# Loading a layer's last keys ahead of its last three values, with the last unit's turned probabilities in the place of the final piece of w_down

## The chip, the cores and the metric

The kernel runs on one core of one Trainium2 chip. TensorE (PE) multiplies, VectorE (DVE) transposes and reduces, ScalarE (ACT) takes exponentials, GpSimd (POOL) makes small tiles, and SyncE (SP) issues every DMA; the DMA engines bring data from HBM to SBUF. The metric is the device time of one execution in microseconds, as the median of several.

## The reference

Two layers, each a decode step of grouped-query attention and a SwiGLU feed-forward block, are applied to `x` of shape (4, 1, 512). Both layers use the same caches and weights:

```
x = x + attention(layernorm(x), k_cache, v_cache, wq, wo)
x = x + swiglu(layernorm(x), w_gate, w_up, w_down)
x = x + attention(layernorm(x), k_cache, v_cache, wq, wo)
x = x + swiglu(layernorm(x), w_gate, w_up, w_down)
```

There are 4 sequences, 32 query heads and 8 key/value heads of width 128, and 8192 cached positions. `attention` is `softmax(q k^T / sqrt(128)) v` followed by `wo`; `swiglu` is `(silu(x w_gate) * (x w_up)) w_down` with 1792 hidden columns. All inputs are bf16. The keys and the values hold 67 MB each, so that the two layers read some 270 MB, against which all weights are small.

## The kernel before, in words

**Units.** A layer has 16 units (`NP`); one unit is a pair of key/value heads of one sequence. Its keys are 4 MB (128 partitions by 16384 columns) and its values as many. Layer 0 takes the units in the order 0 to 15, layer 1 in the order 15, 14, 0, 1, ..., 13 (`order`, line 294), since the keys of unit 15 and the values of 14 and 15 stay in SBUF from one layer to the next (`keep`, line 392). K and V with a number are the keys and values of the unit at that place of its layer.

**Slots.** SBUF has four slots of 4 MB (`kv`, `NSLOT`). Keys, values and, at the end of a layer, the weights of the feed-forward block (`W`) take them in turn. A slot has eight parts. `cmds` (lines 300 to 332) is the list of all loads with their slots. `pump` (line 363) issues them from SP strictly in that order: a load whose slot is not free holds back all that follow. A slot becomes free part by part, as the products that read it are done (`finished`, `freed`). At the end of a layer the order of loads is K14, V13, K15, V14, the two halves of V15, W. In layer 0 W takes the slot of V13, and in layer 1 also the slot of V13. At the beginning of layer 1 the loads go in quarters and halves, so that they can start before a whole slot is free.

**Work on a unit's keys** (`keys`, line 495). DVE transposes each of the eight parts in place (`turn`, line 422). PE then multiplies each part with the placed queries, four products a part (`scores`, line 442), into one of two PSUM banks (`SBK`). When all eight are done come the steps of the softmax: the maximum over positions (`max_p`, line 448), its turn to one row and the reduction to eight heads (`max_t`, lines 452 and 455), the broadcast, bias and exponential (`exps`, lines 462 to 469, into the tile `pb`), the sum and its reciprocal (`total`, lines 478 and 480, into `rl`), and the transposes of the probabilities (`turn_p`, line 475, from `pb` to the tile `pT`).

**Work on a unit's values** (`values`, line 518). Four parts of eight products each (line 530) read `pT` and write one PSUM bank (`OBK`); two parts use up one half of the slot. Then DVE gathers the four quarters of that bank into `acc`, which lies in `pb` (`gather`, lines 546 and 549), PE combines the partitions (line 553), and DVE scales with `rl` (line 555). After the fourth unit of a group of heads, `out_proj` (line 570) multiplies with `wo` and adds to `x`.

**Order of the work.** The program order of all engines is made when the kernel is built. `blocks` holds the products of keys and values, each with a nominal duration, and `drain` (line 487) emits them with a lag behind the transposes. `line` holds the small steps, each with a gap that has to pass in blocks before it is emitted (`advance`). The exponential and what follows wait in `behind` until the values of the unit before are done (line 539), since `pT` and `pb` have one buffer each; `flush` (line 412) emits what is left of a unit's steps before its values. Line 699 sets the order K0, K1, V0, K2, V1, ..., K15, V14, V15. After it come `center`, `deviation` and `ffn`: the gate and up products (line 647), the activation, the down products in three pieces (line 666). The parts of W's slot become free after the gate products, the up products and the down products, and the keys of layer 1 go there.

`_Sync` (line 21) makes the semaphore waits: each operation names what it reads and writes, and waits for the last writers and readers of these names.

Of the kernel before, what the change touches and what calls it, by code (L numbers as in the profile page):

```python
# [103 lines left out]
def bass_interleave_layers__gqa_block_cached__swiglu_ffn__decode_kernel(  # L104
# [40 lines left out]
    with ExitStack() as es:  # L145
# [13 lines left out]
        W_SLOT = (0, 2)  # L159
# [22 lines left out]

        def room(s, a, b):
            return [f"s{s}.{q}" for q in range(a // BW, (b - 1) // BW + 1)]
# [115 lines left out]
        cmds = []  # L300
        us = order[0]
        seq = [K(0, us[0])]
        for i in range(1, NP):
            seq += [K(0, us[i]), V(0, us[i - 1])]
        seq.append(V(0, us[-1]))
        for i, it in enumerate(seq):
            cmds.append((it, i % NSLOT, 0, NB))
        where = {it: s for it, s, _, _ in cmds}
        last = cmds.pop()
        cmds += [(last[0], last[1], 0, NB // 2), (last[0], last[1], NB // 2, NB)]  # L310
        assert where[V(0, NP - 2)] == 2 and where[K(0, NP - 1)] == 1 and where[V(0, NP - 1)] == 3
# [7 lines left out]
        rest = []  # L319
        for i in range(3, NP):  # L320
            rest += [K(1, us[i]), V(1, us[i - 1])]
        rest.append(V(1, us[-1]))
        ring = (0, 3, 1, 2)
        for i, it in enumerate(rest):
            s = ring[i % NSLOT]
            if i in (0, 2):
                cmds += [(it, s, q, q + 2) for q in range(0, NB, 2)]
            elif i == 1 or i == len(rest) - 1:
                cmds += [(it, s, q, q + NB // 2) for q in range(0, NB, NB // 2)]
            else:  # L330
                cmds.append((it, s, 0, NB))
        cmds += [(("W", 1), W_SLOT[1], 0, NB)]

# [4 lines left out]
        def load_weight(name, i=0, s=0):  # L338
# [7 lines left out]
            else:  # L346
                w0 = kvf[:, s * SL:(s + 1) * SL]
                T.dma("sp", w0[:, 0:KT * F].rearrange("p (k f) -> p k f", k=KT),
# [9 lines left out]
                for j, (a, b) in enumerate(WD):  # L358
# [134 lines left out]
        behind = []  # L493

        def keys(L, u, alone, lag):
            def block(q):
# [21 lines left out]
        def values(L, u):  # L518
            gp, b = pair_gb(u)

            def part(i):
                if i == 0:
                    flush(u)
# [225 lines left out]
```

## Time and profile before

| what | value |
| --- | --- |
| median of 3 runs | 660.75 us (660.32 to 662.91) |
| the profiled execution | 663.07 us |
| its span on the core | 661.3 us |
| mean granted TensorE clock | 0.817 |
| PE, DVE, ACT, POOL busy | 65%, 64%, 6%, 2% of the span |
| DMA | 274.44 MB, mean 415 GB/s |
| the main DMA queue's packets | 97.9% of 16 engines' span |
| chain that ended last | DMA 56%, PE 19%, DVE 18%, issue 4% |

The chain that ended last is followed back from the last instruction: at each step it goes to what released that instruction. Its DMA part is the keys (`kvf<-in_A_k_cache_dram`). Times inside the profile count from the start of the span. A row of the timeline gives start, length, engine, line, operation, tiles and count, and in brackets the idle time of the engine before it and what ended it. A row of the windows gives the stretch, its length, the busy time (and count) of PE, PEld, DVE, ACT and POOL, the granted TensorE clock, the DMA share and GB/s.

### The profile page before, as it was taken

Reading aid. Unit: us, or ns where it says so; the run is one execution under the profiler, and the core shown is the slowest. Engines: PE = TensorE matmul, PEld = TensorE weight load, DVE = VectorE, ACT = ScalarE, POOL = GpSimd, SP = SyncE. Lnnn points to the kernel's source line nnn. Section 1 sums busy time; section 2 is a strip of 40 time slices with the busy share of each in tenths; the row PEclk is TensorE's granted clock in tenths of the full one; section 3 lists DMA queues with packets and bytes.
Section 4 is the critical chain, followed back from the end, with each engine's and each line's share of the span. In section 5 each row is a group of like instructions: output and inputs, shape, how many; then the busy total and the mean of one; then the engine's idle time right before and its main releaser. Section 6 shows DMA issues by size and latency. Waiting matters only on the chain.

```text
span 661.3 us, 7677 instructions
## 1 busy us (share of the span) xinstructions
PE 429.4 (65%) x3192; PEld 185.0 (28%) x3192; DVE 420.3 (64%) x701; ACT 38.6 (6%) x107; POOL 10.7 (2%) x43
## 2 busy tenths in 40 slices
PE   2575467465777655577657888677666568765576
PEld 2222123122223222233225342222322123222135
DVE  1675457566677666577644948867756667765673
ACT  1000000000000000000000000000000000000010
POOL 0000000000000000000000000000000000000000
PEclk9995797689887778987675969997767898777886
DMA  9999999999999999999998999999999999999994
GB/s 379 419 428 403 433 429 414 423 436 431 429 431 428 437 428 431 431 429 432 420 406 331 347 426 437 429 435 428 431 430 431 434 427 432 431 431 429 430 411 153
DMA packets 19522, 274.44 MB, mean 415 GB/s; under 512 B 1560, under 2 KB 5920, under 8 KB 9504
## 3 DMA queue, kind: packets, MB, share of 16 engines
q1 hardware_dynamic: 19488, 273.95, 97.9%
q8 instruction: 25, 0.41, 0.3%
q14 instruction: 9, 0.07, 0.0%
HBM read 273.94 MB, written 0.00 MB: 414 GB/s over the span
## 4 chain that ended last, share of the span: by engine, by line
DMA 56%; PE 19%; DVE 18%; issue 4%; another core or an unknown queue 1%; ACT 1%; SPq 0%; POOL 0%; ACTq 0%; DVEq 0%; POOLq 0%
DMA kvf<-in_A_k_cache_dram 56%; PE ps L442 12%; DVE kvf L422 11%; PE ps L530 2%; DVE pT L475 2%; DVE pb L549 2%; PE ps L570 1%; PE ps L647 1%; ACT pb L467 1%; PE ps L462 1%; PE ps L608 1%; PE ps L553 0%; DVE pb L546 0%; PE ps L666 0%
## 5 line engine op out<-in xcount | busy, mean ns | idle before, releaser
L442 PE MATMUL ps<-kvf,zq 128*128 128x512 bf16 x1024 | 306.3, 444 | 183.6 <-DVE kvf L422 179.8
L422 DVE STREAM_TRANSPOSE kvf<-kvf 128x1024 f32<-128x1024 f32 x248 | 293.1, 1216 | 157.0 <-DMA kvf<-in_A_k_cache_dram 156.9
L442 PEld LDWEIGHTS ps<-kvf,zq 128*128 128x128 bf16 x1024 | 97.4, 109 | 336.4 <-DVE kvf L422 231.4
L530 PE MATMUL ps<-kvf,pT 128*32 128x512 bf16 x1024 | 70.5, 399 | 12.3 <-DVE pT L475 12.3
L467 ACT ACTIVATE pb<-ps,tiny 128x512 bf16<-128x512 f32 x32 | 22.0, 687 | 577.2 <-DVE tiny L465 454.5
L475 DVE STREAM_TRANSPOSE pT<-pb 64x512 bf16<-64x512 bf16 x64 | 43.7, 682 | 1.1
L530 PEld LDWEIGHTS ps<-kvf,pT 128*32 128x32 bf16 x1024 | 23.8, 98 | 45.8 <-issue 28.7
L549 DVE SCALAR_TENSOR_TENSOR pb<-ps,tiny,pb 128x128 f32<-128x128 f32 x96 | 33.7, 351 | 3.4
L448 DVE TENSOR_REDUCE tiny<-ps 128x1 f32<-128x512 f32 x32 | 22.0, 689 | 4.7 <-PE ps L442 3.5
L553 PEld LDWEIGHTS ps<-sel,pb 128*128 128x128 f32 x64 | 17.8, 287 | 19.8 <-DVE pb L549 10.6
L455 DVE TENSOR_REDUCE m<-ps 1x8 f32<-1x128 f32 x32 | 8.8, 276 | 19.8 <-PE ps L452 19.8
L433 POOL TENSOR_TENSOR zq<-scr,tiny 128x64 bf16<-128x64 bf16 x32 | 9.6, 299 | 605.2 <-PE ps L442 523.8
L553 PE MATMUL ps<-sel,pb 128*128 128x8 f32 x64 | 12.9, 274 | 7.1 <-DVE pb L549 7.1
L546 DVE TENSOR_SCALAR pb<-ps,tiny 128x128 f32<-128x128 f32 x32 | 10.1, 315 | 9.6 <-PE ps L530 9.6
L478 PE MATMUL ps<-rsm,tiny 128*128 128x8 f32 x64 | 11.6, 254 | 6.0 <-ACT rsm L469 5.8
L478 PEld LDWEIGHTS ps<-rsm,tiny 128*128 128x128 f32 x64 | 10.6, 194 | 17.3 <-ACT rsm L469 16.0
L462 PEld LDWEIGHTS ps<-m,tiny 1*128 1x128 f32 x64 | 10.2, 198 | 17.1 <-issue 15.9
L462 PE MATMUL ps<-m,tiny 1*128 1x8 f32 x64 | 13.1, 274 | 0.2 <-DVE m L455 0.2
L608 PE MATMUL ps<-xn,wq_sb 128*128 128x4 bf16 x256 | 7.9, 166 | 4.8 <-DMA wq_sb<-in_A_wq_dram 4.7
L452 PE MATMUL ps<-identf,tiny 128*1 128x128 f32 x32 | 8.8, 273 | 1.9 <-DVE tiny L448 1.9
L469 ACT ACTIVATE rsm<-head,tiny 128x8 f32<-128x8 f32 x32 | 9.6, 301 | 1.0
L480 DVE RECIPROCAL rl<-ps 128x8 f32<-128x8 f32 x32 | 5.5, 172 | 6.2 <-PE ps L478 6.2
(61 smaller groups left out, 94.3 us busy)
## 6 DMA issues: line engine op xcount, KB each, us to landing
kvf<-in_A_k_cache_dram SPq DMA_DIRECT2D x27, 4096.0 KB, 26.9
kvf<-in_A_v_cache_dram SPq DMA_DIRECT2D x27, 4096.0 KB, 34.0
kvf<-in_A_v_cache_dram SPq DMA_DIRECT2D x6, 2048.0 KB, 26.3
kvf<-in_A_k_cache_dram SPq DMA_DIRECT2D x12, 1024.0 KB, 9.2
wq_sb<-in_A_wq_dram SPq DMA_DIRECT2D x4, 1024.0 KB, 7.9
wo_sb<-in_A_wo_dram SPq DMA_DIRECT2D x4, 1024.0 KB, 28.3
kvf<-in_B_w_gate_dram SPq DMA_DIRECT2D x2, 1792.0 KB, 29.0
kvf<-in_B_w_down_dram SPq DMA_DIRECT2D x4, 768.0 KB, 19.6
```

What stands on the lines that cost most here:

```text
L422: T.op("dve", lambda e: e.transpose(w, w), reads=[f"s{s}.{q}"], writes=[f"s{s}.{q}"])
L442: T.op("pe", lambda e: e.matmul(bank(bk)[:, 0:SW], lhsT=zq[:, z0:z0 + P], rhs=w[:, :, c // 2, :, c % 2], start=(q == 0 and c == 0), stop=( ...
L448: T.op("dve", lambda e: e.tensor_reduce(mx[:], bank(bk)[:, 0:SW], AX.X, ALU.max), reads=[f"pb{bk}"], writes=["mx"])
L462: T.op("pe", lambda e: e.matmul(bank(STEP)[:, 0:H2], lhsT=onesf[0:1, :].to_broadcast([1, P]), rhs=m8[:], start=True, stop=True), reads=["m ...
L467: T.op("act", lambda e: e.activation(pb[:], bank(bk)[:, 0:SW], ACTF.Exp, bias=nm, accum_out=rs), reads=[f"pb{bk}", "nm"], writes=PB + ["rs"])
L475: T.op("dve", lambda e: e.transpose(dst, pb[hp]), reads=["pb"], writes=["pT"])
L478: T.op("pe", lambda e: e.matmul(bank(TOT)[:, 0:H2], lhsT=ones, rhs=rsm[:], start=True, stop=True), reads=["rsm", "onesf"], writes=[f"pb{TO ...
L530: T.op("pe", lambda e: e.matmul(bank(OBK)[j * QB:(j + 1) * QB, :], lhsT=pT[:, t, h, :], rhs=v[:, :, t, :], start=first, stop=stop), reads= ...
L546: T.op("dve", lambda e: e.tensor_scalar(acc, o(0), own[:, 0:1], None, op0=ALU.mult), reads=[f"pb{OBK}", "own"], writes=PB)
L549: T.op("dve", lambda e: e.scalar_tensor_tensor(acc, o(q), own[:, q:q + 1], acc, op0=ALU.mult, op1=ALU.add), reads=[f"pb{OBK}", "own", "pb" ...
L553: T.op("pe", lambda e: e.matmul(bank(CMB)[:, 0:H2], lhsT=acc, rhs=sel[:], start=True, stop=True), reads=["pb", "sel"], writes=[f"pb{CMB}"])
L608: T.op("pe", lambda e: e.matmul(bank(LNB)[:, h * B:(h + 1) * B], lhsT=wq_sb[:, kt, h * Dh:(h + 1) * Dh], rhs=xn[:, kt * B:(kt + 1) * B], s ...
```

## The change

The last keys of a layer, K15, are loaded and multiplied ahead of V13, V14 and V15; before, V13 came ahead of K15 and V14 behind it. The list of loads ends in K14, K15, V13, V14, the halves of V15, W in both layers, and the work in K14, K15, V13, V14, V15 (`todo`). So K15 takes the slot that V13 had, and V13 that of K15; W has the slot of V13 in layer 0 (`W_SLOT` is 1) and of K15 in layer 1 (2). The slots of the loads at the start of layer 1 are renumbered to go with it.

The softmax steps of units 14 and 15 from `exps` on now both stand behind the values of unit 13. Two units' probabilities are then alive at once. Those of unit 15 get a second place: the last 1024 columns of W's slot (`late_pT`), which the last piece of w_down fills at the end of the layer. POOL clears that place, when what lay there is done with, and the last piece of w_down becomes a load of its own (`W+`), which waits for the values of unit 15 and stands on SP ahead of layer 1's first keys. The row of maxima `m8` and the reciprocals `rl` become two each.

```diff
-        W_SLOT = (0, 2)
+        W_SLOT = (1, 2)
...
+        pT_w = TB * NH * QB
+        def late_pT(s):
+            return kvf[:, (s + 1) * SL - pT_w:(s + 1) * SL]
...
-        m8 = sb("m8", [1, H2], FP32)
+        m8 = sb("m8", [1, 2, H2], FP32)
-        rl = sb("rl", [P, H2], FP32)
+        rl = sb("rl", [P, 2, H2], FP32)
...
+        def loads(L, first):
+            us = order[L]
+            seq = []
+            for i in range(first, NP - 1):
+                seq += [K(L, us[i]), V(L, us[i - 1])]
+            seq.insert(len(seq) - 1, K(L, us[NP - 1]))
+            return seq[:-2] + [seq[-2], seq[-1], V(L, us[NP - 2]), V(L, us[NP - 1])]
...
-        cmds += [(("W", 0), W_SLOT[0], 0, NB)]
+        cmds += [(("W", 0), W_SLOT[0], 0, NB), (("W+", 0), W_SLOT[0], NB, NB + 1)]
         us = order[1]
-        cmds += [(K(1, us[1]), 0, 0, 3), (K(1, us[1]), 0, 3, 4), (K(1, us[1]), 0, 4, NB)]
-        cmds += [(K(1, us[2]), 1, q, q + 2) for q in range(0, NB, 2)]
...
-        ring = (0, 3, 1, 2)
...
-        cmds += [(("W", 1), W_SLOT[1], 0, NB)]
+        s = W_SLOT[0]
+        cmds += [(K(1, us[1]), s, 0, 3), (K(1, us[1]), s, 3, 4), (K(1, us[1]), s, 4, NB)]
+        cmds += quarters(K(1, us[2]), 0)
+        seq = loads(1, 3)
+        cmds += placed(seq, (1, 3, 0, 2), {0: quarters, 1: half, 2: quarters, len(seq) - 1: half})
+        cmds += [(("W", 1), W_SLOT[1], 0, NB), (("W+", 1), W_SLOT[1], NB, NB + 1)]
...
+                if name == "W+":
+                    load_wd(w0, len(WD) - 1, ["late"])
+                    return
+                T._wait("pool", T._need((), [f"s{s}.{NB - 1}"]))
+                T.op("pool", lambda e: e.memset(late_pT(s).bitcast(FP32), 0.0), writes=["late"])
                 T.dma("sp", w0[:, 0:KT * F].rearrange("p (k f) -> p k f", k=KT),
...
-                for j, (a, b) in enumerate(WD):
-                    T.dma("sp", w0[:, O_WD + a * D:O_WD + b * D].rearrange("p (m x) -> p m x", x=2 * D),
-                          B_w_down[a * P:b * P, :].rearrange("(m p e) n -> p m (e n)", p=P, e=2), sem_w["wd"][j],
-                          writes=[f"wd{j}"])
+                for j in range(len(WD) - 1):
+                    load_wd(w0, j)
...
+        def pT_of(L, u):
+            if u == order[L][-1]:
+                return late_pT(W_SLOT[L]).rearrange("p (t n x) -> p t n x", n=NH, x=QB), "late"
+            return pT[:], "pT"
...
-                    behind.extend([step(0.9, exps), step(1.0, total), step(0.3, turn_p)])
-                    if alone:
-                        line.extend(behind)
-                        behind.clear()
+                    (line if before is None else behind.setdefault(before, [])).extend(
+                        [step(0.9, exps), step(1.0, total), step(0.3, lambda u: turn_p(L, u))])
...
                 if i == 0:
-                    flush(u)
+                    flush(order[L][-1] if u == order[L][-2] else u)
...
                 if i == 3:
+                    if p_name == "late":
+                        freed(W_SLOT[L], NB, NB + 1)
                     done.add((L, u))
                     line[0:0] = rest_
-                    line.extend(behind)
-                    behind.clear()
+                    line.extend(behind.pop(u, []))
...
-            for i, u in enumerate(us):
+            todo = [("K", 0)]
+            for i in range(1, NP - 1):
+                todo += [("K", i), ("V", i - 1)]
+            todo[-1:] = [("K", NP - 1)] + [("V", i) for i in range(NP - 3, NP)]
+            for kind, i in todo:
+                if kind == "V":
+                    values(L, us[i])
+                    continue
...
-                keys(L, u, i == 0, AHEAD if L and i in (1, 2) else LAG)
-                if i:
-                    values(L, us[i - 1])
-            values(L, us[-1])
+                keys(L, us[i], us[min(i - 1, NP - 3)] if i else None, AHEAD if L and i in (1, 2) else LAG)
```

`load_wd` holds the three lines that issued a piece of w_down before and adds the name `late` to what the last piece writes.

In the program order that follows, PE has the scores of K14 and K15 with nothing of V13 between them, then V13, the combine of unit 13, the broadcast and total of unit 14, those of unit 15, V14, the first half of V15, the combine of unit 14, the second half of V15. In layer 1 the output projection of units 8 to 11, which stood among the scores of K15, stands after the first quarter of V14's products. The number of products, transposes and bytes is the same; POOL has two memsets more.

More of the change, by code (lines that the diff above doesn't have):

```diff
@@ new lines, in bass_interleave_layers__gqa_block_cached__swiglu_ffn__decode_kernel, with placed @@
+        half = lambda it, s: [(it, s, q, q + NB // 2) for q in range(0, NB, NB // 2)]
+        quarters = lambda it, s: [(it, s, q, q + 2) for q in range(0, NB, 2)]
+        def placed(seq, ring, parts):
+            out = []
+            for i, it in enumerate(seq):
+                s = ring[i % NSLOT]
+                out += parts[i](it, s) if i in parts else [(it, s, 0, NB)]
+            return out
+        us = order[0]
+        seq = [K(0, us[0])] + loads(0, 1)
+        assert len(seq) == 2 * NP
@@ L491, in drain, with keys @@
                 advance(t)
-        behind = []
-        def keys(L, u, alone, lag):
+        behind = {}
+        def keys(L, u, before, lag):
             def block(q):
```

62 lines of the change are left out of this document (26 added, 36 removed).

## The prediction

> **What bounds the kernel now.** I read the page first, then the windows of five and three microseconds around the two layer ends, then the chain of waits, then the timeline at both layer ends.
>
> ```profile
> span 661.3 us, 7677 instructions
> GB/s 379 419 428 403 433 429 414 423 436 431 429 431 428 437 428 431 431 429 432 420 406 331 347 426 437 429 435 428 431 430 431 434 427 432 431 431 429 430 411 153
> 350.00:355.00 5.00, 3.36 (x120) 3.20 (x118) 1.72 (x7) 0.81 (x3) 0.00 (x0) 0.50 0.80 281
> 360.00:365.00 5.00, 4.41 (x13) 1.59 (x14) 5.00 (x6) 0.00 (x0) 0.30 (x1) 0.58 0.50 213
> 595.97 28.04 DMA kvf<-in_A_k_cache_dram
> ```
>
> The DMA engines move about 430 GB/s in nearly every slice, so inside a layer the time is bytes over that rate, and the change moves the same bytes. What can be won lies where the DMA idles: after the first layer (share 0.80 and 0.50, so 5 x 0.20 + 5 x 0.50 = 3.5 us of idle) and at the end, where the last slice has 153 GB/s while the chain runs through softmax, the last values and the feed-forward part. The chain of waits enters that end through the last keys, which land at 595.97 + 28.04 = 624.0.
>
> These are the rows of the tail, from the timeline of layer 1 (start, length, engine, line):
>
> ```profile
> 579.14 0.33 SPq L93 DMA_DIRECT2D kvf<-in_A_v_cache_dram  x1
> 604.60 2.37 DVE L422 STREAM_TRANSPOSE kvf<-kvf 128x1024 f32<-128x1024 f32 x2 [6.77 <-DMA kvf<-in_A_k_cache_dram]
> 613.39 3.10 PE L442 MATMUL ps<-kvf,zq 128*128 128x512 bf16 x12
> 614.20 1.18 DVE L422 STREAM_TRANSPOSE kvf<-kvf 128x1024 f32<-128x1024 f32 x1
> 616.00 0.71 DVE L475 STREAM_TRANSPOSE pT<-pb 64x512 bf16<-64x512 bf16 x1
> 619.18 0.38 SPq L93 DMA_DIRECT2D kvf<-in_B_w_gate_dram  x1
> 621.01 23.41 SPq L93 DMA_DIRECT2D kvf<-in_B_w_down_dram  x3
> 624.03 2.37 DVE L422 STREAM_TRANSPOSE kvf<-kvf 128x1024 f32<-128x1024 f32 x2 [5.61 <-DMA kvf<-in_A_k_cache_dram]
> 634.63 0.94 PE L570 MATMUL ps<-oT,wo_sb 128*128 128x4 bf16 x32
> 635.44 1.03 PE L442 MATMUL ps<-kvf,zq 128*128 128x512 bf16 x4
> 636.51 0.69 DVE L448 TENSOR_REDUCE tiny<-ps 128x1 f32<-128x512 f32 x1 [0.16 <-PE ps L442]
> 637.58 1.05 PE L530 MATMUL ps<-kvf,pT 128*32 128x512 bf16 x16
> 637.69 0.28 DVE L455 TENSOR_REDUCE m<-ps 1x8 f32<-1x128 f32 x1 [0.49 <-PE ps L452]
> 641.07 0.17 DVE L465 CUSTOM_DVE_ANT_0 rsm<-ps,head 128x8 f32<-128x8 f32 x1 [0.22 <-PE ps L462]
> 642.49 0.60 PE L478 MATMUL ps<-rsm,tiny 128*128 128x8 f32 x2 [1.46 <-ACT rsm L469]
> 643.25 1.40 DVE L475 STREAM_TRANSPOSE pT<-pb 64x512 bf16<-64x512 bf16 x2
> 644.79 3.25 PE L530 MATMUL ps<-kvf,pT 128*32 128x512 bf16 x32 [1.70 <-DVE pT L475]
> 648.09 0.35 DVE L546 TENSOR_SCALAR pb<-ps,tiny 128x128 f32<-128x128 f32 x1 [3.45 <-PE ps L530]
> 648.48 1.12 DVE L549 SCALAR_TENSOR_TENSOR pb<-ps,tiny,pb 128x128 f32<-128x128 f32 x3
> 649.65 0.39 PE L553 MATMUL ps<-sel,pb 128*128 128x8 f32 x2 [1.61 <-DVE pb L549]
> 652.70 0.89 PE L647 MATMUL ps<-xn,kvf 128*128 128x4 bf16 x28 [0.36 <-DVE pb L589]
> ```
>
> I call the units of a layer by their place, 0 to 15. Before, K15's keys land at 624.03 with DVE idle for 5.6 us ahead of them; their scores end at 636.47 (635.44 + 1.03), V14's products at 638.63, then one softmax chain runs with nothing beside it, and V15 runs from 644.79 to 648.04, which is the point I compare with.
>
> And these are the same places of layer 0, with the issues of V15's halves in layer 1, two rows of landing times (both layer ends show the same 26.7 for V15's halves) and the two Pool rows that the next part needs:
>
> ```profile
> 295.24 17.09 SPq L93 DMA_DIRECT2D kvf<-in_A_v_cache_dram  x3
> 310.75 1.40 DVE L475 STREAM_TRANSPOSE pT<-pb 64x512 bf16<-64x512 bf16 x2
> 314.61 0.38 SPq L93 DMA_DIRECT2D kvf<-in_B_w_gate_dram  x1
> 315.05 20.38 SPq L93 DMA_DIRECT2D kvf<-in_B_w_up_dram  x4
> 335.84 7.20 SPq L93 DMA_DIRECT2D kvf<-in_B_w_down_dram  x3
> 340.36 3.57 PE L530 MATMUL ps<-kvf,pT 128*32 128x512 bf16 x32 [1.70 <-DVE pT L475]
> 350.80 27.51 SPq L93 DMA_DIRECT2D kvf<-in_A_k_cache_dram  x11
> L433 POOL TENSOR_TENSOR zq<-scr,tiny 128x64 bf16<-128x64 bf16 x32 | 9.6, 299 | 605.2 <-PE ps L442 523.8 <-DVE scr L629 81.5
> 352.28 1.33 PEld L647 LDWEIGHTS ps<-xn,kvf 128*128 128x128 bf16 x47 [1.41 <-issue]
> L93 SPq DMA_DIRECT2D kvf<-in_A_v_cache_dram x2: 327/327/327, 612.2 to 616.6; - x2
> kvf<-in_A_v_cache_dram SPq DMA_DIRECT2D x2, 2048.0 KB, 26.7
> kvf<-in_B_w_gate_dram SPq DMA_DIRECT2D x1, 1792.0 KB, 29.0
> L259 POOL MEMSET identf<- 128x128 f32 x1 | 0.2, 205 | 0.3 <-POOLq L734 0.3
> 648.00:651.00 3.00, 1.12 (x33) 0.99 (x30) 1.58 (x5) 0.00 (x0) 0.00 (x0) 0.99 0.89 332
> ```
>
> **The change, part by part.** *K15 loads in V13's place.* In the tail of layer 1 the load issued at 579.14, behind K14's, is now K15's. K14 is there at 604.60 and the old K15 at 624.03, two transfers later, so the transfer between them lands half way, at 614.3. That is before DVE is free: the last transpose of K14 ends at 615.4 and the turned probabilities of unit 13 at 616.71. So the wait for K15 goes away and DVE becomes the limit. Work: eight transposes at 2.37 / 2 = 1.185 make 9.5; one maximum of K14 (0.69) and its small reduction (0.28) lie among them; 616.7 + 10.45 = 627.15. The last transpose of K14 ends at 615.38 and its last score at 616.49, so I add 1.1: scores end at 628.25. V13's products and unit 15's maximum take what V14's took, 636.47 to 638.63, 2.16: they end at **630.4**. In layer 0 the probabilities are turned by 312.15, and the same 13.7 gives **325.9**.
>
> *Two softmax chains in a row, then V14.* From here nothing covers the chain. The first costs what it costs now, 638.63 to 644.65 (643.25 + 1.40), 6.02. The second (bias, exponential, total) goes from 641.07 to 643.09 in the old rows, 2.02; its own transposes lie beside V14 on DVE. V14 starts 8.1 after V13: 638.5 and 334.0. Its 32 products now stand on the path, where before they were covered by the maximum of unit 15: 3.25 to 3.57, taken as 3.4. V15 must then wait, since V14 and V15 share one PSUM bank: the gather is 0.35 + 1.12 and handovers, 1.6. In layer 1 the output projection of units 8 to 11, which ran beside K15's transposes at 634.63, is now issued inside V14's products: 0.94 more on PE, with no cover. V15 starts at 339.0 in layer 0 and at 644.45 in layer 1. Its data are there: the second halves land at about 312.3 + 26.7 = 339.0 and 616.6 + 26.7 = 643.3, and the half needed first lands earlier.
>
> *V15 with the combine of unit 14 in its middle.* Sixteen products cost 1.05 at a full clock and 3.5 / 2 = 1.75 at half; the combine costs 0.39 to 0.60. Both fast: 2.5; both slow: 4.1; the first half fast and the second slow: 3.3. I take the middle, since V14's 3.4 us of steady work raises the clock (granted 0.99 right after the old V15, which had been as long) and the wait for the gather lowers it again. Then V15 ends at 342.3 in layer 0, where it ended at 343.93 (**1.6 gained**, between 0.8 and 2.4), and at 647.75 in layer 1 against 648.04 (**0.3 gained**, between 0.5 lost and 1.0 gained).
>
> By the Trainium skill (TensorE: Matmul & The Clock Gate, "What's actually happening") the array goes to half clock after an idle window of about 3.4 us and back after a busy one, in windows that run free of the kernel. Taken strictly, V14 does not fill a window, V15 stays slow, and both layers take their lower figure, a sum of 0.3 and 660.4; the 0.99 above agrees that one run as long as V14 suffices, and whether it falls into one window no row of before can say.
>
> *What the gain in layer 0 is worth.* The next keys wait for the gate products (350.80). They go out 1.6 earlier, and so does everything up to the second idle stretch; the 3.5 us of idle DMA leave room for 1.6, even for 2.4, so the whole of layer 1 moves by it.
>
> *The weights of the feed-forward part go out later.* W waits for V13 in layer 0 (314.61 becomes 325.9) and for K15's scores in layer 1 (619.18 becomes 628.25). I cost this at nothing: the queue then still holds V15, which lands at 339.0 and 643.3, a cover of 13 and 15 us; w_gate lands at 619.18 + 29.0 = 648.2, ahead of its use at 652.70. SP does sit in long issues (20.38 and 23.41), but in layer 0 it is w_up that takes long and in layer 1 w_down, behind the same amount of queued data; so it waits for room, and a later start meets a queue that has drained. Without that reading it is the slow rival below.
>
> *The last piece of w_down waits for V15* (342.3 and 647.75), and the keys of layer 1 stand behind it on SP. Before, the third issue ended at 343.0 and 644.4. The piece is used after the gate products, which begin 4.7 us after V15, and its 256 KB take 0.6 us at 430 GB/s; the keys wait for the gate products anyway: nothing.
>
> *The fill of the new place* is one Pool memset of 512 columns: 0.205 for 128 columns gives 0.8 by columns; eight times the other row (0.299 for 64) gives 2.4. It starts when V13 (layer 0) or K15's scores (layer 1) end and is needed 8 us later: nothing. The doubled small tiles add no instruction.
>
> Sum: 1.6 + 0.3 = 1.9, between 0.3 and 3.4. The profiled execution took 663.07, 1.8 around its span of 661.3; it becomes 661.2. It stands 2.3 above the median of the runs, 660.75, so I take the same 1.9 off that: **658.9**.
>
> **The rivals.** *The clock stays low (no gain).* Both V14 and V15 run at half clock, the gain is 0.8 - 0.5 = 0.3: 660.4. For it: PE is nearly idle for 8 us ahead of V14. Against it: the old V15 alone raised the clock.
>
> *More than the sum.* The clock is up for all of V15 (3.4), and PE's 1.4 us without a releaser ahead of the up products (352.28), which the same instructions show nowhere in layer 1, falls elsewhere: 3.4 to 4.8, so about 656.7. Against it: two favourable chances in two places.
>
> *SP becomes the bound (slower).* If the long issues are work of their own and not a wait for room, then layer 0's run of issues, 314.61 to 343.04, keeps its 28.4 us and ends at 325.9 + 28.4 = 354.3, and the next keys go out there and not at 350.80: 3.5 later, and the last weights arrive after they are wanted, up to 2 more. Less layer 1's 0.3, 664 to 666, say 664.9. It decides as soon as SP is still issuing when the gate products end. For it: the long rows themselves. Against it: the same kind of load is quick in one layer and slow in the other.
>
> *It doesn't do what it says:* K15 not early enough. DVE is busy until 616.7 and K15 is there at 614.3; 2.4 us of slack speak against it, and the loss would be a part of the gain only.
>
> **How the numbers follow.** Forecast 0.57; low clock or K15 not early, 0.17; more than the sum, 0.15; SP, 0.11. 0.5% is 3.3 us, about what a measurement of this kernel can tell from no change: below 657.4 is faster, above 664.1 slower. The forecast's own range, 657.4 to 660.5, is all "same". Faster gets 0.17 (the third case and a little of the first), slower 0.10 (nearly all of SP), same 0.73. For eight in ten I go from 656.7, the third case's middle, to 661.8, the low clock with the lower side of both layers and 1.4 of spread between runs (the three before differ by 2.6).
>
> **What would show it.** Right: no DVE wait for DMA ahead of the last eight key transposes of a layer; V14 starting some 8 us after V13; V15 ending near 342.3 in layer 0, and near 646.2 in layer 1 (647.75 less the 1.6 of layer 0); the keys of layer 1 issued near 349.2; the weights landing when they do now. Wrong: SP issuing weights past the gate products, DMA below 380 GB/s between V15's landing and the weights', a wait of the second softmax on Pool, or V14 held by its own data.

## The result and the profile after

| | median | range | runs |
| --- | --- | --- | --- |
| before, on the same chip | 661.59 us | 660.32 to 663.83 | 20 |
| changed | 660.01 us | 657.81 to 661.66 | 20 |

The ratio is 0.9971 with a 95% interval of 0.996 to 0.9982: 1.9 us are gained, between 1.2 and 2.6 (the ratio goes by all the runs; the two medians differ by 1.6). That is less than the 0.5% that the prediction named as about what a measurement of this kernel can tell from no change. Both profiled executions lie at the slow end of their runs: the one of before took 663.07 with a span of 661.3, the one after 661.51 with a span of 659.7. So the rows explain 1.6 us.

These are the rows of the page after that answer to those of before, and the two windows after the first layer (stretch, its length, busy time and count of PE, PEld, DVE, ACT, POOL, then granted clock, DMA share and GB/s):

```profile
span 659.7 us, 7650 instructions
GB/s 382 416 428 404 435 414 427 422 441 420 439 421 439 432 427 432 426 440 425 425 403 351 373 425 437 430 434 425 434 429 430 441 420 437 426 433 431 431 407 146
DMA 53%; DVE 28%; PE 10%; issue 4%; SPq 2%; another core or an unknown queue 2%; ACT 0%; POOL 0%; DVEq 0%; ACTq 0%; POOLq 0%
```

```profile
350.00:355.00 5.00, 3.51 (x105) 3.26 (x101) 2.03 (x9) 0.25 (x1) 0.00 (x0) 0.50 0.95 357
360.00:365.00 5.00, 5.00 (x17) 1.93 (x16) 4.21 (x5) 0.00 (x0) 0.00 (x0) 0.69 0.75 274
```

The two slices after the first layer have 351 and 373 GB/s where they had 331 and 347, and the idle DMA time of the two windows is 5 x 0.05 + 5 x 0.25 = 1.5 us where it was 3.5. The gain in time is of this size and lies at this place. The chain that ended last leaves the DMA for good with K14's keys now, where before it was with K15's (595.97 + 28.04 = 624.0). At the end of layer 0 it goes from V13 through SP's issues into the landing of a piece of w_down (start, length, what was waited for):

```profile
337.79 15.14 DMA kvf<-in_B_w_down_dram
575.17 27.41 DMA kvf<-in_A_k_cache_dram
```

From 602.6 to the end of V13 the transposes of K14 and K15 follow each other on DVE. DVE's share of the whole chain went from 18% to 28%, some 60 us. Only about 26 us of that lie at the two layer ends, so the share cannot be put down to K15's keys alone.

The timeline of layer 0 after, engine rows of the steps that the prediction named (L439 are the key transposes, L554 the products with values, L672 gate and up, L691 down, L459 scores):

```profile
300.38 2.37 DVE L439 STREAM_TRANSPOSE kvf<-kvf 128x1024 f32<-128x1024 f32 x2 [5.16 <-DMA kvf<-in_A_k_cache_dram]
312.53 2.37 DVE L439 STREAM_TRANSPOSE kvf<-kvf 128x1024 f32<-128x1024 f32 x2
324.65 1.05 PE L554 MATMUL ps<-kvf,pT 128*32 128x512 bf16 x16
325.79 0.38 SPq L93 DMA_DIRECT2D kvf<-in_B_w_gate_dram  x1
325.84 0.53 POOL L360 MEMSET kvf<- 128x512 f32 x1 [13.12 <-PE ps L554]
326.23 10.09 SPq L93 DMA_DIRECT2D kvf<-in_B_w_up_dram  x4
333.55 3.60 PE L554 MATMUL ps<-kvf,pT 128*32 128x512 bf16 x32
338.87 1.90 PE L554 MATMUL ps<-kvf 128*32 128x512 bf16 x16 [1.71 <-DVE pb L574]
341.22 1.72 PE L554 MATMUL ps<-kvf 128*32 128x512 bf16 x16
348.85 2.38 PE L672 MATMUL ps<-xn,kvf 128*128 128x4 bf16 x84
349.82 4.56 SPq L93 DMA_DIRECT2D kvf<-in_A_k_cache_dram  x3
352.98 1.04 PE L691 MATMUL ps<-pb,kvf 128*128 128x4 bf16 x32 [0.51 <-DMA kvf<-in_B_w_down_dram]
358.75 1.46 PE L459 MATMUL ps<-kvf,zq 128*128 128x512 bf16 x3 [0.79 <-POOL zq L450]
```

The transposes of K15 begin at 312.53 without a wait. V13 ends at 324.65 + 1.05 = 325.70, V14 starts at 333.55, and V15 ends at 341.22 + 1.72 = 342.94, where it ended at 343.93. K14's keys landed 0.35 later in this execution (300.36 for 300.01), so 1.34 us are gained by then. The scores of layer 1's first keys begin at 358.75. Before, they began at the second of these rows; the first stands ahead of the up products:

```profile
352.29 1.41 PE L647 MATMUL ps<-xn,kvf 128*128 128x4 bf16 x47 [1.33 <-issue]
360.59 4.77 PE L442 MATMUL ps<-kvf,zq 128*128 128x512 bf16 x13 [0.79 <-POOL zq L433]
```

So the scores begin 1.84 earlier, or 2.2 with the 0.35: some 0.85 more than at V15. It comes from the gate and up products. Before, 47 of them stood behind 1.33 us of idle time of PE without a releaser (first row); after, the last 84 run in one piece (348.85, 2.38 us). Of these 1.33 the down products give 0.51 back: 32 of them now wait for the second piece of w_down, issued at 337.79 and there at 352.93. It does not come much later than before (issued at 336.90, there at 352.28, so 0.3 later with the 0.35 taken off); the products are ready earlier.

And the same places of layer 1 (L595 is the output projection):

```profile
602.61 2.37 DVE L439 STREAM_TRANSPOSE kvf<-kvf 128x1024 f32<-128x1024 f32 x2 [6.16 <-DMA kvf<-in_A_k_cache_dram]
625.86 0.38 SPq L93 DMA_DIRECT2D kvf<-in_B_w_gate_dram  x1
626.88 1.05 PE L554 MATMUL ps<-kvf,pT 128*32 128x512 bf16 x16
635.59 1.04 PE L554 MATMUL ps<-kvf,pT 128*32 128x512 bf16 x8
636.56 1.01 PE L595 MATMUL ps<-oT,wo_sb 128*128 128x4 bf16 x32
637.50 2.75 PE L554 MATMUL ps<-kvf,pT 128*32 128x512 bf16 x24
641.96 1.90 PE L554 MATMUL ps<-kvf 128*32 128x512 bf16 x16 [1.71 <-DVE pb L574]
644.32 1.90 PE L554 MATMUL ps<-kvf 128*32 128x512 bf16 x16
```

K14's keys are turned 1.99 us earlier than before (602.61 for 604.60): the gain of layer 0 went through layer 1 whole. V15 ends at 646.22, which is 1.82 earlier than before, so 0.17 of it is lost in the tail itself, and some 0.25 more behind V15, which leaves the 1.6 of the whole. V14, the projection and both halves of V15 run at half clock. The windows of these stretches, with the granted clock third from the end, say the same:

```profile
638.00:642.00 4.00, 2.29 (x28) 0.61 (x24) 1.40 (x4) 0.00 (x0) 0.00 (x0) 0.50 0.98 395
642.00:646.00 4.00, 4.00 (x34) 1.43 (x34) 0.18 (x1) 0.00 (x0) 0.00 (x0) 0.50 1.04 392
```

### The profile page after: what moved, and what is told of

Same layout as the page of the kernel before. It is cut to its first block, busy times and chain, and to the rows that moved or that the text cites. A ratio compares the mean times of both kernels' runs of the same rounds, so it can differ in the third digit from the quotient of the medians.

```text
span 659.7 us, 7650 instructions
## 1 busy us (share of the span) xinstructions
PE 431.7 (65%) x3192; PEld 184.4 (28%) x3192; DVE 420.7 (64%) x701; ACT 38.5 (6%) x107; POOL 11.7 (2%) x45
## 4 chain that ended last, share of the span: by engine, by line
DMA 53%; DVE 28%; PE 10%; issue 4%; SPq 2%; another core or an unknown queue 2%; ACT 0%; POOL 0%; DVEq 0%; ACTq 0%; POOLq 0%
DMA kvf<-in_A_k_cache_dram 50%; DVE kvf L439 20%; PE ps L459 5%; DVE pT L499 3%; PE ps L554 2%; DVE pb L574 2%; DMA kvf<-in_B_w_down_dram 2%; SPq L93 2%; DVE pb L571 1%; PE ps L633 1%; PE ps L691 0%; DVE tiny L465 0%; PE ps L578 0%; PE ps L595 0%
## 5 line engine op out<-in xcount | busy, mean ns | idle before, releaser
L459 PE MATMUL ps<-kvf,zq 128*128 128x512 bf16 x1024 | 303.2, 439 | 177.1 <-DVE kvf L439 171.8
L439 DVE STREAM_TRANSPOSE kvf<-kvf 128x1024 f32<-128x1024 f32 x248 | 292.8, 1216 | 145.8 <-DMA kvf<-in_A_k_cache_dram 145.6
L459 PEld LDWEIGHTS ps<-kvf,zq 128*128 128x128 bf16 x1024 | 96.1, 108 | 332.0 <-DVE kvf L439 230.0
L554 PE MATMUL ps<-kvf,pT 128*32 128x512 bf16 x960 | 66.9, 402 | 7.7 <-DVE pT L499 7.7
L499 DVE STREAM_TRANSPOSE pT<-pb 64x512 bf16<-64x512 bf16 x60 | 40.9, 682 | 1.0
L554 PEld LDWEIGHTS ps<-kvf,pT 128*32 128x32 bf16 x960 | 21.9, 99 | 38.7 <-issue 22.6
```

Source lines behind the costliest of these rows:

```text
L439: T.op("dve", lambda e: e.transpose(w, w), reads=[f"s{s}.{q}"], writes=[f"s{s}.{q}"])
L459: T.op("pe", lambda e: e.matmul(bank(bk)[:, 0:SW], lhsT=zq[:, z0:z0 + P], rhs=w[:, :, c // 2, :, c % 2], start=(q == 0 and c == 0), stop=( ...
L499: T.op("dve", lambda e: e.transpose(dst, pb[hp]), reads=["pb"], writes=[name])
L554: T.op("pe", lambda e: e.matmul(bank(OBK)[j * QB:(j + 1) * QB, :], lhsT=p_t[:, t, h, :], rhs=v[:, :, t, :], start=first, stop=stop), reads ...
```

## The experiments

Gains below are one minus the ratio, times the median of the kernel before, run again along with each set of experiments; the bounds come from the ratio's interval. Three questions were open: whether each layer gives what the sum said, what the second place for the probabilities is worth, and what sets V15's end, since its products had run at half clock and not as forecast.

**The change in one layer alone.** Every part of the change asks for its layer; `NEW` is `(0,)` in the first kernel and `(1,)` in the second:

```diff
+        NEW = (0,)
...
-            todo[-1:] = [("K", NP - 1)] + [("V", i) for i in range(NP - 3, NP)]
+            if L in NEW:
+                todo[-1:] = [("K", NP - 1)] + [("V", i) for i in range(NP - 3, NP)]
+            else:
+                todo += [("K", NP - 1), ("V", NP - 2), ("V", NP - 1)]
```

> Layer 0 as in the changed kernel, layer 1 as before. Theory (the gain is made at the end of layer 0: V15 ends about 1.3 earlier there, and PE's 1.33 us without a releaser ahead of the up products falls elsewhere, while layer 1 gives 0.2 to 0.4 back): 2.0 to 2.4 us faster than before, so more than the whole change's 1.9. Rival (both layers gain alike from keys that are there earlier): about 1 us faster.

> Layer 1 as in the changed kernel, layer 0 as before. Theory: V14 with the output projection in it, V15 at half clock and the slow combine use up what the earlier keys bring; 0 to 0.5 us slower than before. Rival: about 1 us faster.

Layer 0 alone took 660.43 us against 661.97, ratio 0.9976 (0.9966 to 0.9987): 1.6 gained (0.9 to 2.3). Layer 1 alone took 660.89, ratio 0.9982 (0.9968 to 0.9995): 1.2 gained (0.3 to 2.1). Layer 0 gives what the prediction's sum had for it. Layer 1 gives something too, and the 0.3 of that sum is the lower edge of its interval. The expectations of these two runs did worse. The 0 to 0.5 of loss for layer 1 is outside its interval, while the rival's gain of about 1 is inside; for layer 0 the interval holds both the theory's 2.0 and the rival's 1. The profiled execution of the second kernel took 662.87, more than the median of before, and its V15 ran at half clock, so its rows cannot show where its gain comes from, and this stays open.

The rows of the first kernel, PE in layer 0 (L561 values, L679 gate and up, L698 down), show what the profiled execution of the changed kernel does not:

```profile
333.08 3.22 PE L561 MATMUL ps<-kvf,pT 128*32 128x512 bf16 x32
338.02 1.05 PE L561 MATMUL ps<-kvf 128*32 128x512 bf16 x16 [1.71 <-DVE pb L581]
339.31 1.05 PE L561 MATMUL ps<-kvf 128*32 128x512 bf16 x16
348.40 1.63 PE L679 MATMUL ps<-xn,kvf 128*128 128x4 bf16 x56 [1.20 <-DMA kvf<-in_B_w_up_dram]
352.23 1.03 PE L698 MATMUL ps<-pb,kvf 128*128 128x4 bf16 x32 [1.09 <-DMA kvf<-in_B_w_down_dram]
```

Layer 0 has the same work in the same order in both kernels, yet here both halves of V15 run at full clock (1.05 each, for 1.90 and 1.72), and V15 ends at 340.36, 2.6 us earlier (2.1 counted from K14's landing, at 299.90 and 300.36). Whether V14 raises the clock in time thus differs from execution to execution. And the earlier end brings little: the up products now wait 1.20 and the down products 1.09 for their weights. Of the 2.1 only 0.3 is left at the first scores of layer 1, which begin at 357.99. From there on it is the landing of the weights that decides, and a quicker tail brings layer 0 little more.

**Without the second place.** The order of loads and values is the changed one, but the probabilities of unit 15 go to the tile `pT`, so that its exponential waits until V14 is done:

```diff
-            if u == order[L][-1]:
-                return late_pT(W_SLOT[L]).rearrange("p (t n x) -> p t n x", n=NH, x=QB), "late"
...
-                    flush(order[L][-1] if u == order[L][-2] else u)
+                    flush(u)
...
-                keys(L, us[i], us[min(i - 1, NP - 3)] if i else None, AHEAD if L and i in (1, 2) else LAG)
+                keys(L, us[i], us[i - 1 if i != NP - 2 else NP - 3] if i else None, AHEAD if L and i in (1, 2) else LAG)
```

> The changed kernel without the second place for the probabilities: unit 15's softmax comes after V14, as it did before. Theory (the second place pays for the early keys: without it the second chain of 6.0 us stands between V14 and V15 in place of the gather's 1.6, less the 2.0 by which V14 starts earlier): V15 ends 2.4 later in each layer than in the changed kernel, which makes it 4 to 5 us slower than that and 2 to 3 us slower than before. Rival (the early keys alone make the gain): within 1 us of the changed kernel.

It took 665.24 us, ratio 1.005 (1.0033 to 1.0068): 3.3 us slower than before and 5.2 slower than the changed kernel, a little more than expected. (The wait of the next paragraph stands in this kernel again, with 1.06 us, so not all of the 5.2 need be the second place's.) Its V14 and V15 in layer 0 (L552):

```profile
331.66 3.60 PE L552 MATMUL ps<-kvf,pT 128*32 128x512 bf16 x32 [1.70 <-DVE pT L497]
341.32 3.60 PE L552 MATMUL ps<-kvf,pT 128*32 128x512 bf16 x32 [1.70 <-DVE pT L497]
```

Between the two lie 6.1 us of softmax, and V15 ends at 344.92. The early keys alone lose, since they leave two softmax chains behind V13 and nothing beside them; only with the second place do the two run as one chain.

**PE's wait without a releaser.** The prediction set 1.33 to 1.4 us ahead of the up products apart as something that might fall elsewhere. Here the kernel before gets 32 tiny products at its start, which shifts all of PE's instructions and nothing else:

```diff
+        for i in range(32):
+            T.op("pe", lambda e: e.matmul(bank(LNB)[:, 0:B], lhsT=ident, rhs=ident[:, 0:B], start=True, stop=True),
+                 reads=["ident"], writes=[f"pb{LNB}"], sig=(i == 31))
```

> The kernel before with 32 tiny products more on PE at its start, while PE waits for the first weights; they write a PSUM bank that is overwritten. Theory: PE's stall of 1.33 us ahead of layer 0's up products comes from where its instructions are fetched (an instruction transfer ends within it), so it moves when 64 PE instructions are put in front: the stall is gone from that place, and the kernel is up to 1.3 us faster, less if it falls on another place of the path. Rival (the stall belongs to the data or to the clock there): the stall stays, no change.

```profile
350.31 2.38 PE L647 MATMUL ps<-xn,kvf 128*128 128x4 bf16 x84
```

The wait is gone from its place: 84 products in one piece, as after the change. With layer 1 alone changed, and without the second place, it stood there again, with 1.61 and 1.06 us. So it is not the products' data that they wait for, and a shift of PE's stream takes it away. The change itself adds no product ahead of this place; why the wait is gone there too stays open. In the time little of it is seen: 661.30 us, ratio 0.9994 (0.9983 to 1.0006), which is 0.4 gained, between 1.1 gained and 0.4 lost. A gain of 1.33 is shut out; a smaller one is possible, and so is none.

**What sets V15's end.** Three edits of the changed kernel, one for each thing that stood in V15's way in layer 1: the output projection inside V14's products, the shared PSUM bank, the half clock. First, the projection goes ahead of unit 15's total, into a wait of PE:

```diff
-                        line.append([0.5, None, lambda: out_proj(gp)])
+                        if u == order[L][-3]:
+                            line.insert(len(line) - 2, [0.0, None, lambda: out_proj(gp)])
+                        else:
+                            line.append([0.5, None, lambda: out_proj(gp)])
```

> The changed kernel with the output projection of units 8 to 11 issued ahead of unit 15's total, where PE waits for ACT some 2.5 us, and not inside V14. Theory (its 1.0 us is on layer 1's path): 0.8 to 1.0 us faster than the changed kernel. Rival (V15 is held by its own data, which land at 641.6): no change.

It took 658.63 us, ratio 0.995 (0.9935 to 0.9964): 3.3 gained over before, so 1.4 more than the change alone (0.2 to 2.6, by the two half intervals added as squares). V14 in layer 1 (L554):

```profile
634.91 3.60 PE L554 MATMUL ps<-kvf,pT 128*32 128x512 bf16 x32
```

It ends at 638.51, 36.8 us after the first transpose of K14 (601.74), where the changed kernel needed 37.6 (640.25 less 602.61). So nearly 0.9 of the projection's 1.0 us was on the path, as the prediction had it. The rest lies within the intervals, and layer 0, whose work is the same, happened to run V15 at full clock in the profiled execution.

Second, V15 writes the bank that held K14's scores, and need not wait for the gather of unit 14 (1.71 us ahead of V15 in the rows above):

```diff
+            ob_ = SBK[turn_of[order[L][-2]]] if u == order[L][-1] else OBK
...
-                    T.op("pe", lambda e: e.matmul(bank(OBK)[j * QB:(j + 1) * QB, :], lhsT=p_t[:, t, h, :], rhs=v[:, :, t, :],
+                    T.op("pe", lambda e: e.matmul(bank(ob_)[j * QB:(j + 1) * QB, :], lhsT=p_t[:, t, h, :], rhs=v[:, :, t, :],
```

> The changed kernel with V15 in the PSUM bank that held K14's scores, so that it need not wait for V14's gather. Theory (layer 0 is held by the landing of the weights, where the down products already wait 0.5 us for DMA, so only layer 1 can gain): V15 follows V14 at once, the wait of 1.7 goes and part of V15 runs at full clock; layer 1 ends 2 to 3 us earlier, layer 0 at most 0.5; 2 to 3.5 us faster than the changed kernel. Rival (both layers are bound by this chain): 4 to 6 us faster.

It took 657.36 us, ratio 0.9933 (0.992 to 0.9947): 4.4 gained over before, 2.5 more than the change alone. V15 in layer 1 (L555):

```profile
639.47 1.74 PE L555 MATMUL ps<-kvf 128*32 128x512 bf16 x16
641.62 1.05 PE L555 MATMUL ps<-kvf 128*32 128x512 bf16 x16
```

It follows V14 at once, and by the second half the clock is up: 1.05 for 1.90. So part of this gain is the clock's again.

Third, the clock. PE gets dummy products of 512 columns among the small softmax steps between V13 and V14, where it waits: 6, 6 and 10 (their result is not read):

```diff
+        def spin(n):
+            for i in range(n):
+                T.op("pe", lambda e: e.matmul(bank(LNB)[:, 0:D], lhsT=wo_sb[:, 0, 0:P], rhs=wo_sb[:, 0, :], start=True, stop=True),
+                     reads=["wo0"], writes=[f"pb{LNB}"], sig=(i == n - 1))
...
+                    if u == order[L][-3]:
...
+                        line.insert(6, [0.0, None, lambda: spin(10)])
+                        line.insert(3, [0.0, None, lambda: spin(6)])
+                        line.insert(1, [0.0, None, lambda: spin(6)])
```

> The changed kernel with 6, 6 and 10 products of 128x512 into an unused PSUM bank between V13 and V14 in each layer, so that PE stays busy through the two softmax chains; the output is the same. Theory (V14, V15 and the combine run at half clock because PE idles ahead of them): V14 takes 2.1 in place of 3.6, V15's halves 1.05 in place of 1.9; layer 1 ends about 3 us earlier, layer 0 hardly, since the weights' landing takes over: 2 to 3.5 us faster than the changed kernel. Rival (the clock does not follow this work, or the added products delay the chain): no gain, or up to 4 us slower.

It took 656.27 us (655.29 to 658.12), ratio 0.9919 (0.9903 to 0.9936): 5.4 gained over before (4.2 to 6.4), 3.5 more than the change alone, the fastest median of all. V14 and V15 in layer 1 (L559), and the window with the granted clock:

```profile
633.99 0.61 PE L559 MATMUL ps<-kvf,pT 128*32 128x512 bf16 x8
635.43 1.48 PE L559 MATMUL ps<-kvf,pT 128*32 128x512 bf16 x24
638.62 1.05 PE L559 MATMUL ps<-kvf 128*32 128x512 bf16 x16 [1.71 <-DVE pb L584]
640.20 1.05 PE L559 MATMUL ps<-kvf 128*32 128x512 bf16 x16 [0.21 <-DMA kvf<-in_A_v_cache_dram]
```

```profile
638.00:642.00 4.00, 2.41 (x34) 1.02 (x34) 1.28 (x5) 0.00 (x0) 0.00 (x0) 1.00 1.01 401
```

V14's 32 products take 2.1 us for 3.8, V15's halves 1.05 each for 1.90, and the second half now waits 0.21 for its own data. That names the next bound: the landing of V15.

**Clock and projection together; all three together.** If V15's landing decides, the projection's 1.0 us should be worth nothing on top of the dummies (6, 6 and 6 here, since the projection fills a part of the wait), and all three edits should not add up. In the expectations below e5 is the kernel with the dummies alone and e6 that with all three edits. The first kernel differs from e5 by this:

```diff
-                        line.insert(6, [0.0, None, lambda: spin(10)])
+                        line.insert(6, [0.0, None, lambda: spin(6)])
...
-                        line.append([0.5, None, lambda: out_proj(gp)])
+                        if u == order[L][-3]:
+                            line.insert(len(line) - 2, [0.0, None, lambda: out_proj(gp)])
+                        else:
+                            line.append([0.5, None, lambda: out_proj(gp)])
```

> The changed kernel with the output projection of units 8 to 11 ahead of unit 15's total, and with 6, 6 and 6 dummy products of 512 columns in TensorE's waits between V13 and V14. It is e5_pe_kept_busy with the projection moved. Theory: with TensorE at full clock, V15 in layer 1 is held by the landing of its second half (it waited 0.2 us for it in e5), so that taking the projection's 0.6 to 1.0 us out of the chain brings nothing more: within 0.5 us of e5's 656.3. Rival: the chain through the total still decides, then about 1 us faster than e5, 655.3.

> The output projection moved, the second bank and 6, 6 and 6 added products together. Theory: V15 becomes bound by the landing of its second half (641.6 in the changed kernel's profile) plus 1.1, against 646.2, and the down products by the last weights (651.9 against a start of 655.1): 3 to 4 us faster than the changed kernel and no more, since the DMA sets the end. Rival (the chain stays the bound): the sum of the three alone.

The first took 657.27 us, ratio 0.9924 (0.9912 to 0.9936), 5.0 gained over before, no better than the dummies alone (5.4 by the ratios; its median is 1.0 higher, twice the half microsecond that was allowed, but not lower as the rival had it). The projection adds nothing that can be seen here. But this kernel has four dummies fewer, and in its profiled execution V15's second half in layer 1 waits 1.26 us for its data and then runs at half clock (1.90), so the run does not part the projection from the clock. The second took 658.06 us, ratio 0.9942 (0.9927 to 0.9957), 3.8 gained over before. That is 1.9 more than the change alone and not the sum of its edits. Its second half of V15 in layer 1 (L560):

```profile
641.51 1.16 PE L560 MATMUL ps<-kvf 128*32 128x512 bf16 x16 [2.80 <-DMA kvf<-in_A_v_cache_dram]
```

With the bank free, the first half runs early, and PE then stands idle for 2.80 us until the second half is there. A kernel with 12 more dummies in that wait shows what this costs:

```diff
+                if i == 1 and u == order[L][-1]:
+                    spin(12)
```

> e6_all_three with 12 more dummy products between V15's first half and the combination of the cores' sums, where TensorE waited 2.8 us for the landing of the second half in e6 and the rest of the kernel ran at half clock. Theory: that wait cost e6 its gain; 0.5 to 1.5 us faster than e6, about 656.5 to 657.5. Rival: e6 lost elsewhere, then within 0.5 us of e6's 658.1.

The kernel runs on one core: what is called the combination of the cores' sums here is the combine of unit 14 over the partitions. The dummies and V15's second half in layer 1 are the first two rows; the last two are V15's second half in layer 0, without the 12 dummies and with them.

```profile
637.62 2.76 PE L543 MATMUL ps<-wo_sb 128*128 128x512 bf16 x12
641.11 1.05 PE L560 MATMUL ps<-kvf 128*32 128x512 bf16 x16 [0.61 <-DMA kvf<-in_A_v_cache_dram]
339.84 1.90 PE L560 MATMUL ps<-kvf 128*32 128x512 bf16 x16 [2.92 <-DMA kvf<-in_A_v_cache_dram]
338.97 1.05 PE L560 MATMUL ps<-kvf 128*32 128x512 bf16 x16 [0.52 <-DMA kvf<-in_A_v_cache_dram]
```

It took 657.20 us, ratio 0.9923 (0.991 to 0.9935), 5.1 gained over before, 1.3 better than without them, as expected, though the two intervals overlap (4.3 to 6.0 and 2.9 to 4.8). With the idle time filled, all three together are back with the others, and not ahead: 656.3, 657.2 and 657.3 are one group, in which the rows show waits for the landing of V15 and, in layer 0, of the weights.

**The clock without the change.** The dummies help the changed kernel; they may help the one before as much. There PE waits between V14 and V15, so the dummies go there, 6, 6 and 7:

```diff
+                    if u == order[L][-2]:
...
+                        line.insert(4, [0.0, u, lambda: spin(7)])
+                        line.insert(3, [0.0, u, lambda: spin(6)])
+                        line.insert(1, [0.0, u, lambda: spin(6)])
```

> The kernel before, with 6, 6 and 7 dummy products of 512 columns between V14 and V15 in each layer, where it turns unit 15's probabilities. If the gain of e5 belongs in part to the clock and not to the change, V15 takes about 2.1 us in place of 3.3 to 3.6 here too, and the kernel is 2 to 3 us faster than before. Rival: V15's landing or the clock's windows leave nothing, within 0.5 us of before.

V15 in the two layers (L535):

```profile
339.90 1.91 PE L535 MATMUL ps<-kvf,pT 128*32 128x512 bf16 x32 [0.18 <-DVE pT L475]
641.82 1.91 PE L535 MATMUL ps<-kvf,pT 128*32 128x512 bf16 x32 [0.18 <-DVE pT L475]
```

It took 658.17 us, ratio 0.9935 (0.9922 to 0.9948): 4.3 gained over before (3.4 to 5.2), more than the 2 to 3 expected, and more than twice what the change gives. V15 takes 1.91 in both layers for 3.57 and 3.25, and ends 41.95 us after K14's landing in layer 0 (341.81 less 299.86) where it needed 43.92. So the larger part of what the dummies and the change give together can be had without the change. Not all of the 4.3 need be the clock's: the dummies also shift PE's stream, and PE's wait ahead of the up products is gone here too:

```profile
347.51 2.57 PE L657 MATMUL ps<-xn,kvf 128*128 128x4 bf16 x84
```

The shift alone gave 0.4 above, and at most 1.1. No run here keeps PE busy in the old order without shifting its instructions.

Reordered and kept busy is 5.4, kept busy alone 4.3. The difference of 1.1 has half an interval of some 1.4 (the two half intervals of 0.165% and 0.13%, added as squares). The two other reordered kernels with dummies, which ran along with this one, point the same way with 5.0 and 5.1. Whether the reordering still pays once the clock is kept up was not settled.

## Why the prediction was right

The predicted time, 658.9 us, took 1.9 off the median shown then, 660.75; measured were 1.9 (1.2 to 2.6). The median itself came out at 660.0, 1.1 above the forecast, since that of before is 661.59 over 20 runs. The forecast was "same", within 0.5%, and so it came. That the sum agrees so closely is in part luck. In the profiled execution V15 gave less than was summed in both layers, and a wait that the sum had left out made up for it. The end of V15 in layer 1, given as near 646.2, came at 646.22 by misses that cancel: the gain brought from layer 0 was 0.4 larger and V14 started 0.9 earlier than summed, against V14 0.3, the gather 0.1 and V15 1.0 longer. By its steps:

- *K15 in V13's place, no wait for its keys.* Right: no DVE wait ahead of the transposes at 312.53, V13 done at 325.70 where 325.9 was said; in layer 1 627.93 (626.88 + 1.05), where 630.4 less the 2.0 of layer 0 makes 628.4.
- *Two softmax chains, V14 8.1 us after V13.* Right: 7.85 in layer 0 (333.55 less 325.70) and 7.66 in layer 1. Without the second place the same order is 3.3 us slower than before, so the change rests on this step.
- *V14 3.4 us, the projection 0.94 on top, the gather 1.6.* Right in kind and close in size: 3.60, 1.01 and 1.71; moving the projection gained about what lay there, and taking V15 off the shared bank gained more (2.5), part of it the clock's.
- *V15 with one half at full clock, 3.3 us.* This size was missed in the profiled execution: 4.07 us in layer 0 and 4.26 in layer 1, the slow side that was named (both slow, 4.1). The execution of the kernel with layer 0 alone shows the other side, 2.34 us. With the projection moved, layer 1 shows one in between, 3.78 us (640.22 to 644.00). Whether 3.3 is a fair value over many executions was not measured. The Trainium skill (TensorE: Matmul & The Clock Gate, "What's actually happening") says that the windows run free of the kernel and that the number of slow products varies between runs; the 2.34 and the 4.07 for the same instructions agree.
- *1.6 from layer 0, 0.3 from layer 1.* The first measured 1.6 (0.9 to 2.3) alone. The second measured 1.2 (0.3 to 2.1) alone, so its size was probably low, though its 0.3 is still at the edge of the interval; the two do not add up to the 1.9 of both, but within their intervals they can.
- *The gain of layer 0 passes whole into layer 1.* Right: 1.99 us at K14's keys. In the profiled execution it was made of 1.34 at V15 and some 0.85 behind it. The second figure was not in the sum: it stood in the rival "more than the sum", as the wait without a releaser. That wait did fall elsewhere, but 0.51 of it was taken back by the weights, and the shifted kernel, in the order of before, puts its worth at 0.4 (between 1.1 gained and 0.4 lost).
- *The weights later, at no cost.* Right in size with one reservation. SP's issue of w_up takes 10.09 us in place of 20.38 although the weights are asked for 11 us later, so the long issues were a wait for room, and the rival in which SP becomes the bound is false: the keys of layer 1 go out at 349.82, not after 354. But the cover was thinner than said: the down products wait 0.51 us for the second piece of w_down here, and in every reordered kernel with a quicker V15 in layer 0 the up products wait 0.3 to 1.6 us and the down products 0.9 to 1.1. The prediction's "up to 2.4" for layer 0 had no room for this.
- *The last piece of w_down behind V15, at no cost.* Right, but only just: it is issued at 343.04, when V15 is done, and is there at 353.60, before at 352.91; no wait for it shows ahead of the last eight down products.
- *Memset at no cost.* Right: 0.53 us beside the gather of unit 13, below both bounds (0.8 and 2.4), and done 7 us ahead of its use.
- *The low-clock rival* (0.8 gained in layer 0, 0.5 lost in layer 1, 660.4) had its condition met in both layers of the profiled execution, and yet this execution is 1.6 us faster than the one of before. Its prices were somewhat low: V15's ends gave 1.34 and -0.17, since V14 started 0.8 and 0.9 earlier than summed, counted from K14's landing; and the 0.85 behind V15 came in addition. By the strict reading of the Trainium skill, which has the same condition, the sum was 0.3; the clock in this execution agrees with it, the time does not, and 1.2 is the lower end of what the runs gave.

## What to carry to other kernels

When a long load is waited for next to a long compute chain, taking the load's place in the queue helps only as far as the chains behind it can run at once; look for the buffer that keeps two of them apart, since the order without it may be slower than what it replaces. Before reordering a tail whose products are few, read the granted clock of its windows: here products that keep TensorE busy through the waits gained 4.3 us in the old order, up to 1.1 of it perhaps by a shift of the instructions, against 1.9 for the reordering. And write down what becomes late next: with a quicker tail it was the landing of the weights and of the last values, which none of the edits tried on the chain moved.

## What was not expected of the hardware

A stretch of dense small products can hold a gap of 1.06 to 1.61 us for which no releaser shows, and 32 products more at the kernel's start take it away from there. The profile's page lists 25 packets of 0.41 MB on the instruction queue, 16 KB each, and one more of them falls between 335 and 360 us in the two kernels without the gap (three, after the change and with the shift) than in the three kernels with it (two):

```profile
q8 instruction: 3, 0.05, 0.8%
```

The Trainium skill (Runtime: NRT & Kernel Launch, "Instruction fetch mechanics") says that instructions come in blocks of 16 KiB, at a cost that is mostly hidden. The size agrees; that the gap is such a block coming late fits the counts, but no run took the block itself away.

Idle time of TensorE can cost something even where it waits for data anyway. In the kernel with all three edits PE is idle for 2.9 and 2.8 us ahead of V15's second half, which in layer 0 then takes 1.90 us. With 12 products whose result nobody reads in that wait it takes 1.05, and 1.3 us of the time come back (0.0 to 2.5, by the two intervals' half widths added as squares).
